# A two-layer expert kernel: side work placed by a count of two engines' time per chunk, and put off a chunk behind a step that feeds the other engine

## The chip, the core and the metric

The kernel runs on one core of a Trainium2 chip. The metric is the device time of one execution in microseconds, from a median of three runs. The engines' names are those of the profile: PE (matmul; PEld is its weight load), DVE (VectorE), ACT (ScalarE), POOL (GpSimd), SP (SyncE, which issues the loads and stores here).

## What is computed

A causal convolution with 7 taps per head (softmaxed), and then two expert layers one after the other, on 8192 tokens of width 192 with a hidden width of 2048, all in float32:

```python
x = _attn_ref(x, weight)             # out[t] = sum_k softmax(weight)[head, k] * x[t - 6 + k]
h = x @ w_in1                        # layer 1
g = h * np.clip(h + 3.0, 0.0, 6.0) / 6.0
x = g @ w_out1
h = x @ w_in2                        # layer 2
g = np.where(h > 0.0, h, np.exp(np.minimum(h, 0.0)) - 1.0)
out = g @ w_out2
```

## The kernel before

**Blocks, layers and chunks.** The tokens are cut into 16 blocks of 512, the hidden width into 16 pieces of 128. A chunk is one piece of one block in one layer, so there are 2 x 16 x 16 = 512 chunks; the code calls them slots (line 578 on) and counts them from 0, and so does this text. The first 32 chunks are layer 1 of blocks 0 and 1, then come blocks 2 to 6 of layer 1 up to chunk 111, and from 112 on a block of layer 2 and a block of layer 1 take turns; from chunk 416 on (blocks 10 to 15) only layer 2 is left. In the code `l` is 0 for layer 1 and 1 for layer 2. Chunk 32 is `BOTH`.

**A chunk's main work.** `mm1` (line 511) makes h = x @ w_in in a PSUM bank; there are three such banks. Float32 values are split in a high and a low part, so x stands as the operands opA (high), opB (low) and opC and opD (the last 64 of the 192 rows, high and low). `gate` (line 535) makes u on ACT and g on DVE; in layer 2 ACT runs twice (u, then its exponential). `split_g` (line 550) makes gh on ACT and gl on DVE, the two parts of g. `mm2` (line 559) adds g @ w_out to accumulators, five chunks later. On ACT and DVE a chunk begins with its u or g, and then holds gh or gl of the chunk before.

**Two streams.** Up to chunk 35 each matmul uses all 128 rows. From chunk 36 (`BOTH + LAG`) on the lower 64 rows and the upper 64 rows of the matmul engine are fed separately, by two generators whose matmuls are emitted alternately (lines 876 to 911); the lower half begins h, the upper half ends it 8 matmuls later. A half takes 10 matmuls for an even chunk and 9 for an odd one, and the other way for the other half. The lower half of chunk s + 3 writes the bank of chunk s, and so waits until g of chunk s has read it. From chunk 36 on the engines execute in the order in which the code emits, within each engine (`tc.manual_schedule`).

**Side work.** All else that ACT and DVE do is split into jobs: decoding and splitting the weights of both layers (`prepare`), the convolution of the later blocks with its taps and the making of opA to opD (`conv`), the split of layer 2's operand (`split_y`), and the sums and stores of results (`second_sum`, `store`). Each is a generator that yields after a step. `run_jobs(s)`, called once a chunk behind gl, first takes every step of a job that is at its last chunk, and then lets each job gain a rate (work left by chunks left) and takes steps while the sum of the gains is over `STEP` (300 units). A unit is about a nanosecond; the class `Meter` counts them for each engine. A step that yields `LATER` is one whose result the other engine needs: from chunk 128 on (`at[0, RA, 0]`) its job takes no further step in that chunk, unless it is at its last chunk.

In `conv_r` (line 339) the steps are: two casts on ACT, two casts on ACT, two subtractions on DVE (opC and opD), `LATER`, and two copies on ACT that read what DVE made. In `split_y` (line 490) they are: the cast of opA on ACT; the cast of the last rows' high part on ACT and opB on DVE; a copy of that high part on ACT and the last rows' subtraction (yr) on DVE; and a copy on ACT that reads what DVE subtracted. `LATER` stands behind each of the first three.

Of the kernel before, what the change touches and what calls it, by code (L numbers as in the profile page):

```python
# [18 lines left out]
LAG = 4  # L19
LAG2 = LAG + 1  # L20
HEAD = 8
RA = 7
# [5 lines left out]
ACT_LOW = range(5, 9)  # L28
R_CUTS = ((4, 4, 8), (8,))
STEP = 300  # L30
NB = 512
HB = NB // 2
SQ = 32
# [23 lines left out]
def conv_moe_moe2(ctx: ExitStack, tc: tile.TileContext, x, weight, w_in1, w_out1, w_in2, w_out2, out):  # L57
# [28 lines left out]
    LO, UP, ALL = slice(0, R), slice(R, P), slice(0, P)  # L86
    NBLK = NT // NB

    vec, act = Meter(nc.vector, 80), Meter(nc.scalar, 90)
# [71 lines left out]
    def split_w(item, f):  # L161

        kind, l, a, e = item
        if kind == "out":
            v = f[:, :(e - a) * D].rearrange("p (f e) -> p f e", f=e - a)
            w = wo[l][:, a:e]
            act.copy(w[:, :, 0:D], v)
            yield  # L170
            for c0, c1, to in ((0, P, 2 * P), (P, D, D)):
                vec.tensor_tensor(out=w[:, :, to:to + c1 - c0], in0=v[:, :, c0:c1],
                                  in1=w[:, :, c0:c1].bitcast(F32), op=ALU.subtract)
            yield
            return
        w = {k: v[:, a * P:e * P] for k, v in wi[l].items()}
        if kind == "in":
            f = f[:, :(e - a) * P]
            act.copy(w["h"], f)
            yield  # L180
            vec.tensor_tensor(out=w["l"], in0=f, in1=w["h"].bitcast(F32), op=ALU.subtract)
        else:
            f = f[:, :(e - a) // 2 * P].rearrange("p (f c) -> p f c", c=P)
            r = w["r"].rearrange("p (f two c) -> p two f c", two=2, c=P)
            for k, h in enumerate((LO, UP)):
                act.copy(r[h, k], f[h])
            yield
            for k, h, o in ((0, LO, UP), (1, UP, LO)):
                vec.tensor_tensor(out=r[o, k], in0=f[h], in1=r[h, k].bitcast(F32), op=ALU.subtract)
        yield  # L190


# [168 lines left out]
    LATER = object()  # L361
# [225 lines left out]
    at = {sl: i for i, sl in enumerate(slots)}  # L587
# [17 lines left out]
    def step(jb, s):  # L605
        w = vec.work, act.work
        said = next(jb[2], jobs)
        done = said is jobs
        if said is LATER and s >= at[0, RA, 0]:
            jb[8] = s  # L610
        cost = vec.work - w[0] + (act.work - w[1]) // 5
        jb[4] += 1
        jb[6] += cost
        jb[7] -= cost
        if done:
            jobs.remove(jb)

    def load(item):
# [3 lines left out]
        lo = {"out": n + 160, "in": n + 80, "r": 2 * n + 160}[kind]  # L622
        return n // 2 + 80 + n + 80 + lo + (2 * n + 180) // 5

    def run_jobs(s):

        def last(jb):
            return jb[0]() - (1 if jb[0]() <= BOTH else 2)

        def rate(jb):  # L630
            if jb[3]:
                return max(jb[5] - jb[6], 0) / max(last(jb) - s, 1)
            need, most = 0, 0
            for k in range(ready[0], len(items)):
                need += load(items[k]) * (1 - min(steps[0], 3) / 4 if k == ready[0] else 1)
                most = max(most, need / max(due(items[k]) - LEAD - 1 - s, 1))
            return most

        for jb in sorted(jobs, key=lambda j: j[0]()):
            while jb in jobs and (s >= last(jb) or not jb[5] and jb[3] and s >= jb[1]):  # L640
                step(jb, s)
        for jb in jobs:
            if s >= jb[1]:
                jb[7] += rate(jb)
        while True:
            going = [j for j in jobs if s >= j[1] and s > j[8]]
            if sum(j[7] for j in going) <= STEP:
                break
            step(max(going, key=lambda j: j[7]), s)

    def whole(*gens):
        for g in gens:
# [5 lines left out]

    def due(item):
        kind, l, a, e = item  # L660
        return at[l, 0, a] + ((LAG, LAG2 - 2)[l] if kind == "out" else 0)

    def when(i):

# [102 lines left out]
    for b in range(2, NBLK):  # L767
        e = at[0, b, 0] - 2
        if b <= RA:
            t = at[0, b - 1, 0]  # L770
            if b > 2:
                t, e = t - 2, e + (b < RA)
            else:
                t += NF // 2
        else:
            t = at[0, b - 1, 0] - 8
            e = at[0, b - 1, NF - 1]
        job(feed(b), 1, t - 8, t - 7)
        job(whole(squares(b), conv(b)), 2 + CONV, t, e, WORK["conv"])
    for b in range(NBLK):  # L780
        e = at[1, b, 0]
# [57 lines left out]
    BOTH = at[0, 2, 0]  # L839
# [55 lines left out]

    drain(whole_rows())
    with tc.manual_schedule():
        ends = {}
        n = {LO: 0, UP: HEAD}
        for half in (LO, UP):  # L900
            for s in range(BOTH + LAG, NS):
                assert half is LO or n[half] > ends[s]
                n[half] += 5 if (half is LO) == (slots[s][2] % 2 == 0) else 4
                if half is LO:
                    ends[s] = n[half]
                n[half] += 5 * (s >= BOTH + LAG2)
        going = [lower_rows(), upper_rows()]
        while going:
            for g in list(going):
                if next(g, jobs) is jobs:  # L910
                    going.remove(g)
        for k in range(B):
            drain(mm2(NS - 1, ALL, (0, 1, 3), slice(k * HB, (k + 1) * HB)))
        last_store(NBLK - 1, *(acc.pop((1, NBLK - 1, up)) for up in (False, True)))
        run_jobs(NS + 9)
# [30 lines left out]
```

## Time and profile before

| what | value |
|---|---|
| time, median of 3 runs (1141.54 to 1142.05) | 1141.55 us |
| the profiled execution, its own time | 1141.55 us |
| its span, first to last instruction | 1139.7 us |
| granted clock of PE, mean | 0.999 |
| PE busy | 1127.6 us (99%) |
| DVE busy | 918.5 us (81%) |
| ACT busy | 935.1 us (82%) |

Busy time of PE is modelled, since matmuls overlap. The list of waits says for each engine whom it waited for, and the timeline gives single instructions in order of time, with the idle time ahead of one in brackets and who ended it. The second number of a row of the timeline is the instruction's own duration; on DVE and ACT the next one can start before its end.

### The profile page before, as it was taken

How to read it: one execution, taken by the hardware profiler on the slowest of the kernel's cores; microseconds unless marked ns; L12 is line 12 of the kernel's file. 1: busy time of each engine (PE TensorE's matmuls, PEld its weight loads, DVE VectorE, ACT ScalarE, POOL GpSimd, SP SyncE). 2: the span in 40 equal slices, each digit the busy share in tenths (PEclk: the TensorE clock that was granted, in tenths of full speed). 3: DMA queues.
4: the chain of work that ended last, by engine and by line, in shares of the span. 5: the costliest groups of instructions: out<-in, count | busy, mean ns of one | idle time of the engine just before them, and what ended most of it. 6: DMA issues, size and time to landing. Idle time of an engine off the chain costs nothing.

```text
span 1139.7 us, 25118 instructions
## 1 busy us (share of the span) xinstructions
PE 1127.6 (99%) x9490; PEld 1065.4 (93%) x9490; DVE 918.5 (81%) x1558; ACT 935.1 (82%) x1699; POOL 44.5 (4%) x491
## 2 busy tenths in 40 slices
PE   8999999999999999999999999999999999999998
PEld 6787989888899999999999999999999999999997
DVE  7998999998887868779687887878867677777675
ACT  8877877778878787887878878787886899899886
POOL 0000000000000000000000000000000000000000
PEclk9999999999999999999999999999999999999999
DMA  6411121010010100101001010000000000000001
GB/s 188 108 53 42 36 49 44 29 29 1 2 29 1 21 10 2 29 1 29 2 7 23 1 29 1 16 15 1 16 1 15 2 1 16 15 15 15 9 7 28
DMA packets 105369, 26.79 MB, mean 24 GB/s; under 512 B 96416, under 2 KB 104096, under 8 KB 105248
## 3 DMA queue, kind: packets, MB, share of 16 engines
q1 hardware_dynamic: 104960, 24.99, 10.3%
q8 instruction: 74, 1.21, 0.4%
q14 instruction: 47, 0.39, 0.1%
q10 hardware_dynamic: 288, 0.20, 0.1%
HBM read 18.87 MB, written 6.29 MB: 22 GB/s over the span
## 4 chain that ended last, share of the span: by engine, by line
PE 92%; ACT 4%; DVE 3%; issue 1%; DMA 0%; ACTq 0%; SPq 0%; DVEq 0%
PE p L573 48%; PE h L527 44%; ACT u L51 1%; DVE g L51 1%; DVE gl L51 1%; DVE acc L51 0%; ACT gh L51 0%; ACT opC L51 0%; ACT xw L51 0%; ACT opD L51 0%; ACT diagl L51 0%; ACT xT L51 0%; DMA x_sq<-in_x_dram 0%; ACT acc L51 0%; DVE s L51 0%
## 5 line engine op out<-in xcount | busy, mean ns | idle before, releaser
L573 PE MATMUL p<-gh,wo 64*128 64x512 f32 (+1 forms) x2976 | 717.2, 386 | 0.0
L573 PE MATMUL p<-gl,wo 64*128 64x512 f32 (+2 forms) x1984 | 601.5, 386 | 0.0
L51 DVE SCALAR_TENSOR_TENSOR g<-u,h 128x512 f32<-128x512 f32 x512 | 350.4, 685 | 184.6 <-ACT u L51 178.2
L573 PEld LDWEIGHTS p<-gh,wo 64*128 64x128 f32 (+1 forms) x2976 | 412.9, 184 | 27.9 <-ACT gh L51 1.1
L51 DVE TENSOR_TENSOR gl<-g,gh 128x512 fp32r<-128x512 f32 x512 | 350.5, 685 | 1.9 <-ACT gh L51 1.6
L51 ACT CAST gh<-g 128x512 fp32r<-128x512 f32 x512 | 311.9, 609 | 9.6 <-DVE g L51 9.2
L51 ACT ACTIVATE u<-h,three 128x512 f32<-128x512 f32 x256 | 176.1, 688 | 107.7 <-PE h L527 105.3
L573 PEld LDWEIGHTS p<-gl,wo 64*128 64x128 f32 (+2 forms) x1984 | 252.6, 160 | 6.7 <-DVE gl L51 0.2
L51 ACT ACTIVATE u<-h 128x512 f32<-128x512 f32 x256 | 152.7, 597 | 57.5 <-PE h L527 56.2
L527 PE MATMUL h<-opA,wi1l 64*128 64x512 f32 x512 | 198.0, 387 | 0.0
L527 PE MATMUL h<-opA,wi1h 64*128 64x512 f32 x512 | 197.9, 386 | 0.0
L527 PE MATMUL h<-opB,wi1h 64*128 64x512 f32 x512 | 197.6, 386 | 0.0
L527 PE MATMUL h<-opA,wi0h 64*128 64x512 f32 (+1 forms) x476 | 183.9, 390 | 2.4 <-DVE g L51 2.1
L527 PE MATMUL h<-opA,wi0l 64*128 64x512 f32 (+1 forms) x476 | 183.3, 388 | 0.0
L527 PE MATMUL h<-opB,wi0h 64*128 64x512 f32 (+1 forms) x476 | 182.7, 387 | 0.0
L51 ACT ACTIVATE u<-u 128x512 f32<-128x512 f32 x256 | 161.9, 633 | 7.6
L527 PE MATMUL h<-opC,wi1r 64*128 64x512 f32 x384 | 148.2, 386 | 0.0
L527 PE MATMUL h<-opD,wi1r 64*128 64x512 f32 x384 | 148.2, 386 | 0.0
L527 PE MATMUL h<-opC,wi0r 64*128 64x512 f32 (+1 forms) x366 | 141.0, 387 | 0.7 <-ACT opC L51 0.6
L527 PE MATMUL h<-opD,wi0r 64*128 64x512 f32 (+1 forms) x366 | 140.8, 387 | 0.0
L51 DVE SCALAR_TENSOR_TENSOR acc<-xT,taps,acc 128x256 f32<-128x256 f32 (+1 forms) x180 | 106.8, 603 | 0.1
L527 PEld LDWEIGHTS h<-opA,wi0h 64*128 64x128 f32 (+1 forms) x476 | 87.6, 184 | 11.3 <-DVE g L51 6.5
(108 smaller groups left out, 1220.5 us busy)
## 6 DMA issues: line engine op xcount, KB each, us to landing
raw<-in_moe_w_out_dram SPq DMA_DIRECT2D x16, 384.0 KB, 3.2
out_dram<-z SPq DMA_DIRECT2D x180, 32.0 KB, 1.7
x_sq<-in_x_dram SPq DMA_DIRECT2D x112, 32.0 KB, 2.1
raw<-in_moe_w_in_dram SPq DMA_DIRECT2D x7, 512.0 KB, 3.9
raw<-in_moe_w_in_dram SPq DMA_DIRECT2D x8, 256.0 KB, 4.0
xr_sq<-in_x_dram SPq DMA_DIRECT2D x56, 32.0 KB, 2.1
x_sb<-in_x_dram SPq DMA_DIRECT2D x4, 128.0 KB, 2.9
raw<-in_moe_w_in_dram SPq DMA_DIRECT2D x4, 128.0 KB, 3.2
```

The costliest lines, as they stand in the source:

```text
L51: return fn(*args, **kw)
L527: mm = nc.tensor.matmul(h, k, m[half], start=low and i == 0, stop=high and i == len(todo) - 1)
L573: nc.tensor.matmul(p[:n, cols], k[:, :n], m[half, cols], start=first and not end and k is not w0l, stop=end == 1 and (last and cols.stop = ...
```

## The change

Five things are changed. `booked` counts for DVE and for ACT the units of a chunk, with what is over a chunk's 2153 (`SLOT`) carried on, and `full` stops the second loop of `run_jobs` once either has that much; the first loop, for jobs at their last chunk, does not ask it. `LATER` counts from chunk 36 on and not from 128. The weights of layer 2 are due 12 chunks earlier (`SOON`). The two subtractions of a wi1r item become two steps. And `run_jobs` runs once more, for chunk 35, at the head of the two streams.

```diff
--- before.py
+++ after.py
@@ -28,6 +28,8 @@
 ACT_LOW = range(5, 9)
 R_CUTS = ((4, 4, 8), (8,))
 STEP = 300
+SLOT = 2153
+SOON = 12
 NB = 512
 HB = NB // 2
 SQ = 32
@@ -187,6 +189,8 @@
             yield
             for k, h, o in ((0, LO, UP), (1, UP, LO)):
                 vec.tensor_tensor(out=r[o, k], in0=f[h], in1=r[h, k].bitcast(F32), op=ALU.subtract)
+                if l == 1 and k == 0:
+                    yield
         yield
 
 
@@ -606,7 +610,7 @@
         w = vec.work, act.work
         said = next(jb[2], jobs)
         done = said is jobs
-        if said is LATER and s >= at[0, RA, 0]:
+        if said is LATER and s >= BOTH + LAG:
             jb[8] = s
         cost = vec.work - w[0] + (act.work - w[1]) // 5
         jb[4] += 1
@@ -621,6 +625,11 @@
         n = (e - a) * {"out": D, "in": P, "r": R}[kind]
         lo = {"out": n + 160, "in": n + 80, "r": 2 * n + 160}[kind]
         return n // 2 + 80 + n + 80 + lo + (2 * n + 180) // 5
+
+    booked = [(e, [0, 0]) for e in (vec, act)]
+
+    def full(s):
+        return s >= BOTH + LAG and any(b[0] + e.work - b[1] >= SLOT for e, b in booked)
 
     def run_jobs(s):
 
@@ -636,6 +645,8 @@
                 most = max(most, need / max(due(items[k]) - LEAD - 1 - s, 1))
             return most
 
+        for e, b in booked:
+            b[:] = max(b[0] - SLOT, 0) + e.work - b[1] if s >= BOTH + LAG else 0, e.work
         for jb in sorted(jobs, key=lambda j: j[0]()):
             while jb in jobs and (s >= last(jb) or not jb[5] and jb[3] and s >= jb[1]):
                 step(jb, s)
@@ -644,9 +655,11 @@
                 jb[7] += rate(jb)
         while True:
             going = [j for j in jobs if s >= j[1] and s > j[8]]
-            if sum(j[7] for j in going) <= STEP:
+            if sum(j[7] for j in going) <= STEP or full(s):
                 break
             step(max(going, key=lambda j: j[7]), s)
+        for e, b in booked:
+            b[:] = b[0] + e.work - b[1], e.work
 
     def whole(*gens):
         for g in gens:
@@ -658,7 +671,7 @@
 
     def due(item):
         kind, l, a, e = item
-        return at[l, 0, a] + ((LAG, LAG2 - 2)[l] if kind == "out" else 0)
+        return at[l, 0, a] + ((LAG, LAG2 - 2)[l] if kind == "out" else 0) - l * SOON
 
     def when(i):
 
@@ -895,6 +908,7 @@
 
     drain(whole_rows())
     with tc.manual_schedule():
+        run_jobs(BOTH + LAG - 1)
         ends = {}
         n = {LO: 0, UP: HEAD}
         for half in (LO, UP):
```

The matmuls stand in the same order. What moves on ACT and DVE, first at chunk 442 to 445. ACT before, from u of chunk 442 (u twice, gh, then opC copied from opD) to u of chunk 445:

```order
L51 ACTIVATE u<-h 128x512
L51 ACTIVATE u<-u 128x512
L51 CAST gh<-g 128x512
L51 CAST opC<-opD 64x512
L51 ACTIVATE u<-h 128x512
L51 ACTIVATE u<-u 128x512
L51 CAST gh<-g 128x512
L51 ACTIVATE u<-h 128x512
L51 ACTIVATE u<-u 128x512
L51 CAST gh<-g 128x512
L51 CAST opD<-opC 64x512
L51 ACTIVATE u<-h 128x512
```

ACT now, from u of chunk 443:

```order
L53 ACTIVATE u<-h 128x512
L53 ACTIVATE u<-u 128x512
L53 CAST gh<-g 128x512
L53 CAST opD<-yr 64x512
L53 ACTIVATE u<-h 128x512
L53 ACTIVATE u<-u 128x512
L53 CAST gh<-g 128x512
L53 CAST opC<-opD 64x512
L53 CAST opD<-opC 64x512
L53 ACTIVATE u<-h 128x512
```

The copy of opD from opC has moved next to the copy of opC from opD, into chunk 444. DVE there, before, chunks 442 to 444:

```order
L51 SCALAR_TENSOR_TENSOR g<-u,h 128x512
L51 TENSOR_TENSOR gl<-g,gh 128x512
L51 TENSOR_TENSOR opC<-yr,opD 64x512
L51 SCALAR_TENSOR_TENSOR g<-u,h 128x512
L51 TENSOR_TENSOR gl<-g,gh 128x512
L51 SCALAR_TENSOR_TENSOR g<-u,h 128x512
```

Now, from g of chunk 443 to g of chunk 445:

```order
L53 SCALAR_TENSOR_TENSOR g<-u,h 128x512
L53 TENSOR_TENSOR gl<-g,gh 128x512
L53 TENSOR_TENSOR opB<-y_10208,opA 128x512
L53 SCALAR_TENSOR_TENSOR g<-u,h 128x512
L53 TENSOR_TENSOR gl<-g,gh 128x512
L53 TENSOR_TENSOR opC<-yr,opD 64x512
L53 SCALAR_TENSOR_TENSOR g<-u,h 128x512
```

The subtraction opC, which lies between the two copies of ACT, has moved from chunk 442 to chunk 444. The same holds 16 and 32 chunks earlier and 16, 32 and 48 later, with opC and opD exchanged at every second one; at 412 the first cast of the high part stands in chunk 410.

The second place is chunks 139 to 141, where the convolution of block 8 (64x256, acc) and the split of layer 2's block 1 (64x512, yr) end. ACT before, from u of chunk 139:

```order
L51 ACTIVATE u<-h,three 128x512
L51 CAST gh<-g 128x512
L51 ACTIVATE u<-h,three 128x512
L51 CAST gh<-g 128x512
L51 CAST opC<-opD 64x512
L51 ACTIVATE u<-h,three 128x512
L51 CAST gh<-g 128x512
L51 CAST opD<-opC 64x256
L51 CAST opC<-opD 64x256
L51 ACTIVATE u<-h,three 128x512
```

Now, from the casts behind u and gh of chunk 139:

```order
L53 CAST opD<-acc_4439 64x256
L53 CAST opC<-acc_4439 64x256 x2
L53 CAST opD<-acc_4439 64x256
L53 ACTIVATE u<-h,three 128x512
L53 CAST gh<-g 128x512
L53 CAST opC<-yr 64x512
L53 CAST opD<-opC 64x512
L53 CAST opC<-opD 64x512
L53 ACTIVATE u<-h,three 128x512
L53 CAST gh<-g 128x512
L53 CAST opD<-opC 64x256
L53 CAST opC<-opD 64x256
```

The four casts of the convolution have come into chunk 139, and the last copies of both splits now follow what they read from at once.

DVE there, before, from opB of chunk 138 to g of chunk 140:

```order
L51 TENSOR_TENSOR opB<-acc_4229,opA 128x512
L51 TENSOR_TENSOR opD<-yr,opC 64x512
L51 SCALAR_TENSOR_TENSOR g<-u,h 128x512
L51 TENSOR_TENSOR gl<-g,gh 128x512
L51 TENSOR_TENSOR opC<-acc_4231,opD 64x256
L51 TENSOR_TENSOR opD<-acc_4231,opC 64x256
L51 SCALAR_TENSOR_TENSOR g<-u,h 128x512
```

Now, from g of chunk 140 to g of chunk 142:

```order
L53 SCALAR_TENSOR_TENSOR g<-u,h 128x512
L53 TENSOR_TENSOR gl<-g,gh 128x512
L53 TENSOR_TENSOR opB<-y_1230,opA 128x512
L53 TENSOR_TENSOR opD<-yr,opC 64x512
L53 SCALAR_TENSOR_TENSOR g<-u,h 128x512
L53 TENSOR_TENSOR gl<-g,gh 128x512
L53 TENSOR_TENSOR opC<-acc_4439,opD 64x256
L53 TENSOR_TENSOR opD<-acc_4439,opC 64x256
L53 SCALAR_TENSOR_TENSOR g<-u,h 128x512
```

The subtraction opD on yr and the copy from it were two chunks apart and are in chunk 140; opC and opD on acc and the copies from them were two chunks apart and are in chunk 141.

The third place is the first chunks of the two streams. DVE before, chunks 37 and 38:

```order
L51 SCALAR_TENSOR_TENSOR g<-u,h 128x512
L51 TENSOR_TENSOR gl<-g,gh 128x512
L51 SCALAR_TENSOR_TENSOR acc_1149<-xT_1096,taps,acc_1149 128x512
L51 TENSOR_TENSOR yr<-s_1223,yr 64x512
L51 SCALAR_TENSOR_TENSOR g<-u,h 128x512
L51 TENSOR_TENSOR gl<-g,gh 128x512
L51 SCALAR_TENSOR_TENSOR acc_1151<-xT_1118,taps,acc_1151 128x256
L51 TENSOR_TENSOR wi1r<-xw,wi1r 64x4x128 x2
L51 SCALAR_TENSOR_TENSOR g<-u,h 128x512
```

Now, from gl in chunk 36 to g of chunk 39:

```order
L53 TENSOR_TENSOR gl<-g,gh 128x512
L53 SCALAR_TENSOR_TENSOR acc_1149<-xT_1096,taps,acc_1149 128x512
L53 TENSOR_TENSOR wi1r<-xw,wi1r 64x4x128
L53 SCALAR_TENSOR_TENSOR g<-u,h 128x512
L53 TENSOR_TENSOR gl<-g,gh 128x512
L53 TENSOR_TENSOR yr<-s_1231,yr 64x512
L53 SCALAR_TENSOR_TENSOR acc_1151<-xT_1119,taps,acc_1151 128x256
L53 SCALAR_TENSOR_TENSOR g<-u,h 128x512
L53 TENSOR_TENSOR gl<-g,gh 128x512
L53 SCALAR_TENSOR_TENSOR acc_1149<-xT_1096,taps,acc_1149 128x512
L53 TENSOR_TENSOR wi1r<-xw,wi1r 64x4x128
L53 SCALAR_TENSOR_TENSOR g<-u,h 128x512
```

One wi1r subtraction has moved from chunk 38 to chunk 36, and yr and the taps have changed places.

At chunks 60, 76, 92 and 121 opC and opD on acc stood on DVE before, with the copies from them on ACT in the same chunk at the first three; they stand at 61, 77, 93 and 124 now, with the copies in the same chunk at all four. At 77 and 124 opB stands right ahead of them. The same pairs stood two or three chunks apart at 171, 203 and so on up to 363 and 365, and are in one chunk now (173, 205, 237, 269, 301, 333 and 365).

## Rows read from the trace of the kernel before

**Rows 1.** Busy time by stretch, core 0: us, PE, PEld, DVE, ACT, POOL, PEclk, DMA, GB/s

```profile
99.00:309.00 210.00, 208.12 (x1811) 183.39 (x1812) 191.42 (x342) 167.38 (x311) 8.79 (x96) 1.00 0.12 28
309.00:1128.00 819.00, 819.00 (x7230) 803.81 (x7228) 631.79 (x1021) 681.92 (x1216) 33.45 (x380) 1.00 0.07 12
```

**Rows 2.** Waits, 99 to 309 us: engine, line, waited for, total us, times, longest

```profile
PEld h L527 <- DVE g L51: 5.5, 10, 1.2
...
ACT opD L51 <- DVE opC L51: 3.5, 3, 1.2
```

**Rows 3.** Timeline of PE: start us, us, engine, line, op, tiles; eight first matmuls

```profile
106.69 0.39 PE L527 MATMUL h<-opA,wi0h 64*128 64x512 f32 x1
...
116.73 0.39 PE L527 MATMUL h<-opA,wi0h 64*128 64x512 f32 x1
...
155.49 0.39 PE L527 MATMUL h<-opA,wi0h 64*128 64x512 f32 x1
...
165.30 0.39 PE L527 MATMUL h<-opA,wi0h 64*128 64x512 f32 x1
...
395.62 0.39 PE L527 MATMUL h<-opA,wi0h 64*128 64x512 f32 x1
...
981.33 0.39 PE L527 MATMUL h<-opA,wi1h 64*128 64x512 f32 x1
...
983.60 0.39 PE L527 MATMUL h<-opA,wi1h 64*128 64x512 f32 x1
...
989.94 0.39 PE L527 MATMUL h<-opA,wi1h 64*128 64x512 f32 x1
```

**Rows 4.** Timeline of PE at chunk 64 (in brackets: idle before, by whom ended)

```profile
160.82 0.50 PE L527 MATMUL h<-opA,wi0h 64*128 64x512 f32 x1 [0.80 <-DVE g L51]
...
161.16 0.40 PE L527 MATMUL h<-opB,wi0h 64*128 64x512 f32 x1
```

**Rows 5.** Timeline of DVE, chunks 60 and 61

```profile
156.82 0.69 DVE L51 SCALAR_TENSOR_TENSOR g<-u,h 128x512 f32<-128x512 f32 x1 [1.26 <-ACT u L51]
...
158.03 0.41 DVE L51 TENSOR_TENSOR opC<-acc,opD 64x256 fp32r<-64x256 f32 x1
...
160.08 0.69 DVE L51 SCALAR_TENSOR_TENSOR g<-u,h 128x512 f32<-128x512 f32 x1 [0.53 <-ACT u L51]
```

**Rows 6.** Timeline of ACT, chunks 60 to 62

```profile
158.47 0.41 ACT L51 CAST opD<-opC 64x256 fp32r<-64x256 f32 x1 [1.18 <-DVE opC L51]
...
159.35 0.69 ACT L51 ACTIVATE u<-h,three 128x512 f32<-128x512 f32 x1
...
160.45 0.69 ACT L51 ACTIVATE u<-h,three 128x512 f32<-128x512 f32 x1
```

**Rows 7.** Timeline of ACT, chunks 441, 442, 444 and 445

```profile
977.95 0.60 ACT L51 ACTIVATE u<-h 128x512 f32<-128x512 f32 x1
...
980.15 0.59 ACT L51 ACTIVATE u<-h 128x512 f32<-128x512 f32 x1
...
984.30 0.60 ACT L51 ACTIVATE u<-h 128x512 f32<-128x512 f32 x1
...
986.10 0.62 ACT L51 CAST opD<-opC 64x512 fp32r<-64x512 f32 x1
986.74 0.60 ACT L51 ACTIVATE u<-h 128x512 f32<-128x512 f32 x1
```

**Rows 8.** Timeline of DVE, chunks 442 and 445

```profile
981.43 0.69 DVE L51 SCALAR_TENSOR_TENSOR g<-u,h 128x512 f32<-128x512 f32 x1
...
982.64 0.68 DVE L51 TENSOR_TENSOR opC<-yr,opD 64x512 fp32r<-64x512 f32 x1
...
988.04 0.69 DVE L51 SCALAR_TENSOR_TENSOR g<-u,h 128x512 f32<-128x512 f32 x1 [1.16 <-ACT u L51]
```

**Rows 9.** Timeline of DVE, chunks 37 and 38

```profile
105.73 0.69 DVE L51 SCALAR_TENSOR_TENSOR g<-u,h 128x512 f32<-128x512 f32 x1 [0.86 <-ACT u L51]
...
110.14 1.39 DVE L51 TENSOR_TENSOR wi1r<-xw,wi1r 64x512 fp32r<-64x512 f32 x2
```

## Prediction

> **What bounds the kernel now.** I read the busy time by stretch first, then the waits of the matmul engine, then its cadence, then the order in time around one wait. From 309 us to 1128 us PE is busy in all of 819.00 us, and from 99 us to 309 us it has 1.88 us idle, with DVE at 191 of 210 us [rows 1]. So the end is set by PE's count of matmuls, which the change leaves as it is, and by the moments at which PE waits. [rows 2] says who makes it wait in the two streams: g on DVE (5.5 us of weight-load waits), and ACT in turn stands 3.5 us in three waits for a DVE result, opC.
>
> The cadence gives what is lost. The first matmul of chunk 172's lower half starts at 395.62, that of chunk 444 at 981.33: 272 chunks in 585.71 us, 2.1533 us each [rows 3]. At the same rate the 404 chunks from chunk 40 (106.69) would take 869.95 us; they took 874.64. So **4.69 us are lost in the two streams**, all of it before chunk 172: 1.43 from chunk 40 to 44 (10.04 us for 4 chunks), 1.20 from chunk 62 to 66 (9.81), the other 2.06 in the rest. That is the most that better placed side work can give: 0.41%.
>
> How one loss comes about stands in [rows 4 to 6], chunk 60. ACT has u and gh done, then wants to copy opD from opC. DVE makes opC only after g and gl: g at 156.82, opC at 158.03 for 0.41 us. ACT stands 1.18 us, starts the copy at 158.47 (0.03 us after opC's end), and the next u follows at 159.35: **2.53 us after g**. That delays g of chunk 61 to 160.08, its end to 160.77, and the lower half of chunk 64, which needs the same bank of the three, starts at 160.82, 0.05 us later. After it the next matmul comes 0.34 us on where the cadence is 0.23 (2.1533 over 9.5 matmuls): a restart of some 0.12 us with every stall.
>
> How much lateness PE bears: g of chunk 445 starts at 988.04 for 0.69 us, and the bank is wanted by chunk 448 at 989.94 [rows 3, 8]: 1.21 us. That u was itself 0.17 us late (2.44 us after the one before, where an even chunk takes 981.33 to 983.60, 2.27 us [rows 3, 7]). So an odd chunk of layer 2 has 1.21 + 0.17 - 0.05 = **1.33 us to spare**. In layer 1 g comes 0.73 us after u (159.35 to 160.08) and not 1.30 (986.74 to 988.04): 1.33 + 0.56 = 1.89 for odd chunks, and 0.23 more, 2.12, for even ones, since an odd chunk takes 2.04 (two take 4.31).
>
> **The change part by part.** It issues the same instructions: the matmuls stand in the same order, and one pair of the wi1r subtractions is parted. What moves is side work on DVE and ACT, and some loads on SP's queue; the list of which [rows 2] are two lines names no DMA in that stretch: nothing for these.
>
> *Chunks 36 to 43.* Before, DVE waits 0.86 us for u of chunk 37, since ACT has two wi1r casts and another in chunk 36, and then two wi1r subtractions (1.39 us) stand together in chunk 38 [rows 9]. Now ACT has nothing but u and gh in chunk 36. DVE's chunks 36 to 38 hold other steps of the same size: one wi1r each in 36 and 38, a wide tap where a narrow one and a decode stood. So g of chunk 39 comes the 0.86 us earlier, and of the 1.43 us some 0.5 stay; 0.1 to 0.6 is open, and I take **0.4**.
>
> *The couplings of blocks 3 to 6.* The step that feeds ACT is put off a chunk, but a step at its last chunk is taken whatever was said, and so only the one of chunk 43 becomes free. Those of chunks 60, 76 and 92 come back at 61, 77 and 93. At 61 and 93 u is 2.53 us after g where it would be 2.04 - 0.73 = 1.31: 1.22 us late, with 0.1 to 0.5 brought along, under 2.12: nothing, so that the 1.20 us behind chunk 60 goes. At 77 opB stands ahead of opC (0.60 more): 3.13 - 1.31 = 1.82 late, with 0 to 0.6 of DVE's own; then chunk 78 holds g, gl, wi1r and a transpose (3 x 0.60 + 0.70 = 2.5 us against 2.27): 2.1 to 2.7 late against 1.89. I take the middle, 0.5, and a restart: **0.6 us**.
>
> *The booked count.* It stops side work at 2153 units a chunk, but what is due is put in all the same, so DVE's sum over chunks 62 to 71 stays 0.1 to 0.2 us a chunk over the slot. From the 1.3 us of chunk 62 it may reach the 1.89 at chunk 67: 0 to 0.6, taken as **0.3**.
>
> *Chunk 124 (layer 2).* Block 7's opB, opC, opD and both copies from them now stand in one chunk: u is 3.13 us after g, where it would be 2.27 - 1.30 = 0.97. 2.16 - 1.33 = 0.83, and a restart: **0.9 us**.
>
> *Chunks 140 and 141.* Before, no ACT copy there waits for its own chunk's DVE step. Now chunk 139 has four half-width copies on ACT, 1.10 (159.35 to 160.45, u and gh) + 4 x 0.44 (158.47 to 159.35 has two) = 2.86 us against 2.04: 0.82 late. Chunk 140 has opB, a full-width opD on DVE and the copy from it: 0.60 + (1.21 + 0.68 + 0.03 + 0.64) = 3.16 us from g to u [rows 7, 8], where 2.27 - 0.73 = 1.54 is normal: 2.44 late against 1.89. Chunk 141 adds 2.53 - 1.31: 3.66 late against 2.12. PE loses 1.54 us and two restarts: **1.8 us**.
>
> *The last six blocks.* For blocks 10 to 15 the split of layer 2's operand stood in chunks 441, 442 and 444 (and 16 further on or back): DVE's opC at 982.64, ACT's copy from it at 986.10, two chunks later, and nobody waits. Now DVE's subtraction, the copy that it needs next to it and the copy from its result are all in chunk 444; their sizes stand in [rows 7, 8]. u of chunk 445 comes 1.21 + 0.68 + 0.03 + 0.64 = 2.56 us after g, where 0.97 is normal: 1.59 late. The high part's copy in chunk 443 adds 0.16 (2.20, as from 977.95 to 980.15, against 2.04) in chunks 444 and 476; in 428, 460 and 492 it is of the 0.64 us kind (986.10 to 986.74) and not of the 0.52 us one, 0.28; in 412 none. Less 1.33 that is 0.42 twice, 0.54 three times and 0.26: 2.7 us, and six restarts, 0.7: **3.4 us in a stretch that loses nothing now**.
>
> *Seven more* (173, 205, ... 365) put opC, opD and their copies in one chunk: 1.22 + 0.3 late against 2.12, nothing.
>
> **The sum.** 0.4 + 0.6 + 0.3 + 0.9 + 1.8 + 3.4 = 7.4 us lost after, 4.69 before: +2.7 us. The profiled execution took 1141.55 us, 1.85 more than its span of 1139.7, and that is the median of the three runs too. 1141.55 + 2.7 = **1144.3 us**, slower by 0.24%. The ends: each of the ten new or kept stalls 0.15 us kinder, and the three open terms at their lower ends, make 5.0 lost and 1141.9; each 0.2 us longer, and the open terms at their upper ends, make 10.2 and 1147.0.
>
> **Rivals.** *The late six fit.* Their lateness, 1.59 to 1.87, is over the spare 1.33 by only 0.26 to 0.54. If DVE and ACT are some 0.3 us quicker there (gl does not wait for gh, the copy's start overlaps), most of these stalls go with their restarts: 3.4 falls to 0.5, 4.5 lost in all, 1141.55 - 0.2 = 1141.4: not slower. It decides from some 0.25 us a chunk on. Against it: the 2.53 us chain shows no such overlap. *The wait for a result goes away.* If a put-off step bought its chunk everywhere, as the change says, all but some 1 us of the 4.7 goes: 1141.55 - 3.7 = 1137.9, faster. Against it: the built order has opC and its copy in one chunk at 61, 77, 93, 124 and 141. *DVE's steps do not overlap.* If a step behind a wait on another engine starts only at the end of the one ahead, 0.69 apart and not 0.60, each chain is 0.17 to 0.26 longer; over the ten stalls that is 2 us more: 1146.3. Against it: from g at 981.43 to opC at 982.64, with gl between, are two steps of 0.60 us, though the instructions take 0.69 [rows 8].
>
> [...]
>
> **How the numbers follow.** A measurement of this kernel tells about 0.2%, 2.3 us, from no change. The forecast's case (the late six stall as worked out) has 0.66, the six that fit 0.22, the gain 0.05, the longer chains 0.07. The forecast's own range is 1142.4 to 1146.2 and lies on both sides of the bound at 1143.8; I give 0.45 of its 0.66 to slower. With the longer chains slower has 0.52, faster 0.04, the rest 0.44. The range takes in half of the six that fit and the longer chains' lower part: 1141.3 to 1146.2.
>
> **What would show it.** In the changed kernel's trace: waits of ACT for DVE's opC or opD, some nineteen of 0.7 to 2 us and not three; PE waits for g at about 921, 955, 990, 1025, 1060 and 1095 us, each some 0.4 us, where PE has none now; two close together at about 336 us, 0.5 and 1 us; the wait for u of chunk 37 gone; PE's wait for g of chunk 61, 0.80 us at 160.82, gone [rows 4]. The forecast is wrong if PE is busy without a gap from 400 us on, or if the lateness at 139 to 141 is taken up by DVE having begun opC earlier than its place in the order says. If the late six show and the total is still level, the early part has gained more than I allow.

## The result: 0.62% slower, and the profile after

The changed kernel takes **1148.88 us** (median of 6 runs, 1148.45 to 1149.78) and the kernel before 1141.85 (6 runs, 1141.54 to 1142.84): a ratio of 1.0062, interval 1.0049 to 1.0075. The prediction had the side right and the size not: 1144.3, with 1146.2 as its upper end. The profiled execution took 1148.89 us, its span is 1147.2.

PE's busy time and the busy time by stretch (the columns of [rows 1]) are these; the first line is of the page, the other two of the view by stretch:

```profile
PE 1132.0 (99%) x9490; PEld 985.3 (86%) x9490; DVE 916.8 (80%) x1558; ACT 933.5 (81%) x1699; POOL 44.4 (4%) x491
```

```profile
99.00:309.00 210.00, 207.70 (x1797) 190.71 (x1797) 187.01 (x332) 164.02 (x304) 8.60 (x95) 1.00 0.11 26
309.00:1128.00 819.00, 816.15 (x7180) 708.50 (x7178) 629.67 (x1023) 676.47 (x1210) 33.25 (x377) 1.00 0.07 12
```

Before, PE had no idle time in the second stretch [rows 1]; now it has 2.85 us. DVE and ACT do the same work. The waits changed as a list shows, first of 99 to 317 us, then of 317 to 1136 (engine, line, waited for, total us, times, longest):

```profile
PEld h L531 <- DVE g L53: 5.1, 10, 1.4
ACT opD L53 <- DVE opC L53: 4.7, 4, 1.4
ACT wo L53 <- DVE xw L53: 2.9, 2, 2.5
PE h L531 <- DVE g L53: 1.6, 3, 0.9
PEld h L531 <- ACT opC L53: 1.1, 2, 0.9
...
ACT opD L53 <- DVE opC L53: 12.5, 15, 1.2
PEld h L531 <- DVE g L53: 6.3, 8, 1.1
ACT opC L53 <- DVE opD L53: 4.5, 7, 0.9
```

Where [rows 2] had three waits of ACT for opC there are 26 now for opC or opD, 22 of them after 317 us; 19 take 0.79 to 1.43 us, which are the prediction's "some nineteen", and the rest under 0.3. Two kinds the prediction did not have: ACT for the decoded weight xw, and PE for the operand opC itself.

**Where the time went.** PE's timeline gives the first matmul of the lower half at chunks 40, 44, 72, 84, 96, 104, 130, 148, 412 and 498, which answers to [rows 3]:

```profile
107.10 0.39 PE L531 MATMUL h<-opA,wi0h 64*128 64x512 f32 x1
...
116.23 0.39 PE L531 MATMUL h<-opA,wi0h 64*128 64x512 f32 x1
...
177.00 0.39 PE L531 MATMUL h<-opA,wi0h 64*128 64x512 f32 x1
...
204.69 0.39 PE L531 MATMUL h<-opA,wi0h 64*128 64x512 f32 x1
...
231.19 0.39 PE L531 MATMUL h<-opA,wi0h 64*128 64x512 f32 x1
...
250.17 0.39 PE L531 MATMUL h<-opA,wi0h 64*128 64x512 f32 x1
...
307.00 0.39 PE L531 MATMUL h<-opA,wi0h 64*128 64x512 f32 x1
...
347.53 0.39 PE L531 MATMUL h<-opA,wi1h 64*128 64x512 f32 x1
...
916.15 0.39 PE L531 MATMUL h<-opA,wi1h 64*128 64x512 f32 x1
...
1105.07 0.39 PE L531 MATMUL h<-opA,wi1h 64*128 64x512 f32 x1
```

Each difference less 2.15335 us a chunk (585.71 / 272, the prediction's rate) is what that stretch lost: 231.19 to 250.17, say, are 18.98 us for 8 chunks that need 17.23, so 1.75. The table has the same for before and for the profiled execution of each experiment; the last column is the median of the timed runs. The loss is more than PE's idle time in the views, which counts from the modelled end of the matmul before and leaves out the slow restart: at chunk 448, shown below, it is 0.19 us where the loss is 0.53, and the matmul from opB behind it comes 0.34 us on (995.21 to 995.55), where in the pair before the stall it came 0.22 on (994.38 to 994.60). The spans of the two profiles differ by 7.5 us: 7.05 are this loss, and 0.4 lie before chunk 0, where the programs are the same. In all 14 profiles chunk 0 begins between 13.55 and 14.66 us; from there to chunk 40 all 14 take 93.08 to 93.18 us, so that spread is no work of the change, and the lost time is compared first and the medians second.

| us lost in chunks | 40-44 | 44-72 | 72-84 | 84-96 | 96-104 | 104-130 | 130-148 | 148-412 | 412-498 | sum | median |
|---|---|---|---|---|---|---|---|---|---|---|---|
| before | 1.42 | 1.21 | 0.64 | 0.51 | 0.13 | 0.78 | 0 | 0 | 0 | 4.68 | 1141.85 |
| predicted | 0.4 | 0.3 | 0.6 | 0 | 0 | 0.9 | 1.8 | 0 | 3.4 | 7.4 | 1144.3 |
| after | 0.52 | 0.47 | 1.85 | 0.66 | 1.75 | 0.85 | 1.77 | 0.13 | 3.72 | 11.73 | 1148.88 |
| e1 late steps put off early, alone | 1.43 | 0.63 | 0.07 | 0.52 | 0 | 0.81 | 0 | 0 | 0 | 3.44 | 1140.58 |
| e2 no count | 0.52 | 0 | 0.73 | 0 | 0.40 | 0.91 | 0 | 0 | 0 | 2.55 | 1140.19 |
| e3 bound 2500 | 0.57 | 0.02 | 0.85 | 0.07 | 0 | 1.07 | 0.04 | 0 | 0 | 2.62 | 1139.50 |
| e4 layer 2's split early | 0.57 | 0.51 | 1.88 | 1.72 | 0.11 | 0.79 | 1.40 | 0 | 0 | 6.98 | 1144.18 |
| e5 six coupled in before | 1.42 | 1.18 | 0.63 | 0.52 | 0.17 | 0.79 | 0 | 0 | 4.37 | 9.08 | 1146.68 |
| e6 conv parted | 0.53 | 0.64 | 0.70 | 0.22 | 0 | 0 | 0.75 | 0 | 3.74 | 6.57 | 1144.00 |
| e7 weights parted | 0.03 | 0.43 | 1.81 | 0.31 | 0.03 | 0.78 | 1.73 | 0.05 | 3.80 | 8.96 | 1145.96 |
| e8 bound 2350 | 0.57 | 0.61 | 0.59 | 0.07 | 0.07 | 0.10 | 0.35 | 0 | 0 | 2.36 | 1140.14 |
| e9 count alone | 0 | 1.29 | 1.27 | 1.23 | 2.09 | 7.44 | 7.72 | 0.13 | 3.78 | 24.95 | 1160.31 |
| e10 weights not early | 0.03 | 0.66 | 0.94 | 0.27 | 0 | 2.70 | 6.56 | 0.12 | 3.78 | 15.06 | 1154.27 |
| e11 wi1r parted, alone | 0.77 | 1.79 | 0.63 | 1.84 | 0.13 | 0.79 | 0 | 0 | 0 | 5.93 | 1143.32 |
| e12 all three mended | 0 | 0 | 0.27 | 0.91 | 0 | 0.29 | 0.28 | 0 | 0 | 1.74 | 1138.73 |

**One of the six late stalls**, chunks 444 to 448 of the timelines of ACT, DVE and PE:

```profile
991.11 0.62 ACT L53 CAST opC<-opD 64x512 fp32r<-64x512 f32 x1
992.53 0.62 ACT L53 CAST opD<-opC 64x512 fp32r<-64x512 f32 x1 [0.80 <-DVE opC L53]
993.17 0.60 ACT L53 ACTIVATE u<-h 128x512 f32<-128x512 f32 x1
```

```profile
990.62 0.69 DVE L53 SCALAR_TENSOR_TENSOR g<-u,h 128x512 f32<-128x512 f32 x1
...
991.82 0.68 DVE L53 TENSOR_TENSOR opC<-yr,opD 64x512 fp32r<-64x512 f32 x1
994.47 0.69 DVE L53 SCALAR_TENSOR_TENSOR g<-u,h 128x512 f32<-128x512 f32 x1 [1.97 <-ACT u L53]
```

```profile
995.21 0.50 PE L531 MATMUL h<-opA,wi1h 64*128 64x512 f32 x1 [0.19 <-DVE g L53]
...
995.55 0.40 PE L531 MATMUL h<-opB,wi1h 64*128 64x512 f32 x1
```

u of chunk 445 comes 2.55 us after g of 444 (the prediction said 2.56), g follows 1.30 later and ends at 995.16, and PE starts 0.05 after it. In [rows 7, 8] the copy from opC stood two chunks after it, and PE ran through.

**Two stalls that were not forecast as they came.** Chunk 96 on ACT and DVE, and PE at chunk 100:

```profile
238.73 0.51 ACT L53 CAST wo<-xw 128x384 fp32r<-128x384 f32 x1 [2.52 <-DVE xw L53]
...
239.59 0.67 ACT L53 ACTIVATE u<-h,three 128x512 f32<-128x512 f32 x1
```

```profile
236.98 0.65 DVE L53 SCALAR_TENSOR_TENSOR g<-u,h 128x512 f32<-128x512 f32 x1
237.55 0.68 DVE L53 TENSOR_TENSOR gl<-g,gh 128x512 fp32r<-128x512 f32 x1
238.15 0.55 DVE L53 SCALAR_TENSOR_TENSOR xw<-xw,cw 128x384 int32<-128x384 int32 x1
...
240.30 0.69 DVE L53 SCALAR_TENSOR_TENSOR g<-u,h 128x512 f32<-128x512 f32 x1 [1.33 <-ACT u L53]
```

```profile
241.04 0.49 PE L531 MATMUL h<-opA,wi0h 64*128 64x512 f32 x1 [0.93 <-DVE g L53]
```

It is the same coupling in another job: DVE's decoding step and the ACT copy from it stand in one chunk, and u behind the copy comes 2.61 us after g, 1.30 later than the prediction's normal 1.31. That alone would fit in its 2.12 us to spare. But g of chunk 96 was late already: it ended at 237.63, and PE took that bank for chunk 99 at 237.88, so only 0.20 us of the 2.12 were left (0.25 less the hand-over of 0.05). And chunk 80, the first of block 5, on ACT and on PE:

```profile
195.26 0.41 ACT L53 CAST opD<-opC 64x256 fp32r<-64x256 f32 x1 [1.43 <-DVE opC L53]
195.72 0.40 ACT L53 CAST opC<-opD 64x256 fp32r<-64x256 f32 x1
```

```profile
196.17 0.50 PE L531 MATMUL h<-opC,wi0r 64*128 64x512 f32 x1 [0.48 <-ACT opC L53]
...
197.90 0.39 PE L531 MATMUL h<-opA,wi0h 64*128 64x512 f32 x1
```

PE waits here for the copies of chunk 77 themselves: chunk 80 multiplies by opC, which is ready at 196.12. Chunk 81 begins at 197.90, 1.07 us late.

### The profile page after: what moved, and what is told of

Same layout as the page of the kernel before. It is cut to its first block, busy times and chain, and to the rows that moved or that the text cites. A ratio compares the mean times of both kernels' runs of the same rounds, so it can differ in the third digit from the quotient of the medians.

```text
span 1147.2 us, 25110 instructions
## 1 busy us (share of the span) xinstructions
PE 1132.0 (99%) x9490; PEld 985.3 (86%) x9490; DVE 916.8 (80%) x1558; ACT 933.5 (81%) x1699; POOL 44.4 (4%) x491
## 3 DMA queue, kind: packets, MB, share of 16 engines
q8 instruction: 74, 1.21, 0.4%
## 4 chain that ended last, share of the span: by engine, by line
PE 92%; ACT 4%; DVE 3%; issue 1%; ACTq 0%; DVEq 0%
PE p L577 47%; PE h L531 44%; ACT u L53 2%; DVE g L53 1%; DVE gl L53 1%; PE psc L330 1%; ACT opC L53 0%; DVE opD L53 0%; ACT opD L53 0%; ACT gh L53 0%; DVE opC L53 0%; DVE acc L53 0%; ACT xw L53 0%; ACT xT L53 0%; DVE wi1r L53 0%
## 5 line engine op out<-in xcount | busy, mean ns | idle before, releaser
L577 PE MATMUL p<-gh,wo 64*128 64x512 f32 (+1 forms) x2976 | 708.2, 387 | 0.1
L577 PE MATMUL p<-gl,wo 64*128 64x512 f32 (+2 forms) x1984 | 591.1, 386 | 0.0
L577 PEld LDWEIGHTS p<-gh,wo 64*128 64x128 f32 (+1 forms) x2976 | 391.9, 184 | 45.5 <-ACT gh L53 1.1
L577 PEld LDWEIGHTS p<-gl,wo 64*128 64x128 f32 (+2 forms) x1984 | 241.2, 160 | 25.4 <-DVE gl L53 0.2
L531 PEld LDWEIGHTS h<-opA,wi1h 64*128 64x128 f32 x512 | 94.2, 184 | 12.7 <-DVE g L53 6.3
L53 DVE SCALAR_TENSOR_TENSOR acc<-xT,taps,acc 128x256 f32<-128x256 f32 (+1 forms) x180 | 104.2, 601 | 0.1
```

Of the source, the lines that this page charges most:

```text
L53: return fn(*args, **kw)
L531: mm = nc.tensor.matmul(h, k, m[half], start=low and i == 0, stop=high and i == len(todo) - 1)
L577: nc.tensor.matmul(p[:n, cols], k[:, :n], m[half, cols], start=first and not end and k is not w0l, stop=end == 1 and (last and cols.stop = ...
```

## The experiments

**Is it the count, or the early put-off?** The theory: the bound holds steps back till the last chunk of their job, where they are taken together. e1 is the kernel before with one line changed; e2 is the changed kernel in which the bound is never reached; e3 has `SLOT = 2500`.

```diff
-        if said is LATER and s >= at[0, RA, 0]:
+        if said is LATER and s >= BOTH + LAG:
```

> The kernel before with one part of the change: a step that says 'a chunk later' is put off from the start of the two streams on (chunk 36) and not from chunk 128 on; no booked count, no parting of the wi1r pair, no earlier weights. Theory (the count is at fault): without the count a step is taken when its rate asks for it, well ahead of its last chunk, so the put-off gets its chunk everywhere: no ACT copy waits for opC of its own chunk at 60, 76, 92, PE's 1.2 us behind chunk 60 go, the 1.4 us of chunks 36 to 43 stay: 1139.0 to 1140.6 us, faster than before. Rival (the early put-off itself is what costs): waits of ACT for opC at 61, 77 and 93 as in the changed kernel and losses at 80 to 83 and 97 to 102: 1143 to 1146 us.

```diff
-        return s >= BOTH + LAG and any(b[0] + e.work - b[1] >= SLOT for e, b in booked)
+        return False and any(b[0] + e.work - b[1] >= SLOT for e, b in booked)
```

> The changed kernel without its booked count (the bound is never reached; the put-off from chunk 36, the parted wi1r pair and the earlier weights stay). Theory (the count holds rated steps back to their last chunk, where the DVE step and the copy from it are taken together): all the couplings go, and with them the losses at 416 to 496 (3.7 us), 144 to 146 (1.8), 128/129 (0.8), 97 to 102 (1.7) and most of 80 to 83 (1.7); what is left is 1 to 2.5 us: 1138.5 to 1140.5 us, faster than before. Rival (put-off early): the losses before chunk 128 stay, about 5 us: 1143.5. Rival (bunched work: wherever the steps go, a chunk of DVE or ACT overflows): new stalls of the same sum, 1146 to 1149.

> The changed kernel with one number changed: the bound of the booked count is 2500 a chunk and not 2153, which is its length at the pace of the matmuls. Theory (the bound as such makes the couplings, since layer 1's conv and sums fill it): with 16% more room no copy stands in one chunk with the DVE step before it, and the time is that of the kernel without the count, 1138.5 to 1140.5 us. Rival (it is not the bound, but that steps are counted and taken in another order): 1147 to 1149 us.

All three are faster than before: 1140.58 (ratio 0.9989, 0.9980 to 0.9998), 1140.19 (0.9985, 0.9976 to 0.9994) and 1139.50 us (0.9979, 0.9970 to 0.9988). What e2's trace leaves of the list of waits from 99 to 309 us, as far as PE waits for DVE's g, and of the stretch behind it:

```profile
PEld h L531 <- DVE g L53: 2.7, 5, 0.8
PE h L531 <- DVE g L53: 0.6, 2, 0.4
```

```profile
309.00:1128.00 819.00, 819.00 (x7230) 803.82 (x7228) 631.79 (x1021) 681.78 (x1217) 33.45 (x380) 1.00 0.07 12
```

No wait of ACT for opC or opD of the same chunk is left in either stretch, and PE is busy in all of the second. So the count makes the couplings, and costs 11.73 - 2.55 = 9.2 us; the early put-off alone gains 1.24. e3 says that it is the bound's size. How 2153 is filled can be counted from `Meter` (512 units and 90 for a full-width step of ACT, 80 for one of DVE): a chunk of layer 2 has three such steps on ACT, 1806 units, and one copy more makes 2408; in layer 1 conv and sums fill DVE or ACT. The rated steps then wait, and the loop for last chunks takes them without asking.

**Is a copy behind its own chunk's DVE step the whole price?** e4 lets the split of layer 2's operand begin two chunks ahead of its last one, a step a chunk (`jb[3]` is a job's number of steps; layer 1's sums have 4 too, so its line frees them as well, and the last six blocks have none of these); e5 has no count, and makes only the six late couplings in the kernel before.

```diff
             while jb in jobs and (s >= last(jb) or not jb[5] and jb[3] and s >= jb[1]
+                                  or jb[3] == 4 and s > jb[8] and s >= last(jb) - 2):
```

> The changed kernel, count and all; only the split of layer 2's operand is taken from two chunks ahead of its last chunk on, a step a chunk where it says 'later', and no more all at once in the last chunk. Theory (each late stall is a DVE step and the ACT copy from it in one chunk): the six stalls at 416 to 496 go, 3.7 us, and at 144 the part that chunk 140 adds, 0.5 to 1.0 us; the conv's couplings at 77, 124 and 141 stay with their losses: 1144.0 to 1145.0 us. Rival (PE waits there since ACT or DVE have too much in the chunk, wherever the steps stand): the six stalls move to the chunks beside and stay: 1148 to 1149 us.

```diff
         vec.tensor_tensor(out=lo[h], in0=yr[h], in1=hi[h].bitcast(F32), op=ALU.subtract)
-        yield LATER
+        if b < 10:
+            yield LATER
```

> The kernel before, with no count and nothing else of the change; only for blocks 10 to 15 the split of layer 2's operand has its last put-off taken out, so that DVE's subtraction and the ACT copy from it stand in one chunk (410, 426, ... 490) and not in two. Theory (a copy behind its own chunk's DVE step is the whole price): six stalls of PE at chunks 414, 430, ... 494, 0.4 to 0.8 us each with the restart, 3.4 to 4.5 us in all: 1145.3 to 1146.3 us, and the couplings of 60, 76, 92 as before. Rival (the late steps of the changed kernel cost since the DVE step, the copy before it and the forced chunk come on top of each other, and a lone coupling fits in the slack of 1.33 us): 1141.9 to 1142.9 us.

In e4 the six stalls are gone (3.72 to 0). The sum fits the expectation, but not term by term: 144 to 146 gave back only 0.37 of the 0.5 to 1.0, and the weight's coupling of chunk 96 moved to 80 in the built order, which saves 1.64 at 96 to 104 and costs 1.06 at 84 to 96. The early sums of layer 1 moved it: with the line narrowed to the split, the code emits that step at 96 as before. In e5 six stalls appear out of nothing: 4.37 us, at the upper end of the expectation (its median is 0.4 above it). One of them, on ACT and PE:

```profile
985.48 0.62 ACT L51 CAST opD<-opC 64x512 fp32r<-64x512 f32 x1 [0.80 <-DVE opC L51]
986.13 0.60 ACT L51 ACTIVATE u<-h 128x512 f32<-128x512 f32 x1
```

```profile
988.16 0.50 PE L528 MATMUL h<-opA,wi1h 64*128 64x512 f32 x1 [0.19 <-DVE g L51]
```

The rows repeat those of chunk 444 above: the same 0.80 us on ACT, the same 0.19 on PE. A coupling in an even chunk of layer 2 is enough by itself. In an odd chunk of layer 1 it is not: ACT waits 1.18 us in each of the seven pairs from 173 on, and chunks 148 to 412 lose 0.13 us in all.

**What are the losses before chunk 148?** e6 parts the conv's steps (the line of e4 with `jb[3] > 8` and `last(jb) - 1`); e7 parts the weights' (with `not jb[3]`, `last(jb) - 1`, and the second `yield` of `decode` saying `LATER`). That `LATER` does nothing, in e7 or in e12: `decode` runs inside `counted`, which yields nothing on, so `run_jobs` never sees it. What e7 really does is to take the weights' last steps one chunk earlier; in its trace no copy of a weight stands in one chunk with its xw any more.

> The changed kernel, count and all; only the conv's job may be taken from one chunk ahead of its last chunk on, up to its 'later', so that opC and opD on DVE and the ACT copies from them stand in two chunks in every block. The split of layer 2's operand stays as it is. Theory: ACT no longer waits for opC at 61, 77, 93, 124, 141, and the losses at 80 to 83 (1.7 us, of which 1.07 are PE waiting for the operand itself), at 128/129 (0.8) and most of 144 to 146 (1.8) go, and with the other order of the weights those of 97 to 102 (1.7); the six late stalls (3.7 us) stay: 6.0 us lost, 1143.2 us, 1142.5 to 1144.2. Rival (the early losses come from DVE's side work being too much for chunks 62 to 102, whatever the coupling): 4 us of them stay, 1146 to 1147 us.

> The changed kernel, count and all; only the weights' job says 'later' after DVE's second step of the decode (xw) and may be taken from one chunk ahead of its last chunk on, so that the ACT copy of the decoded weight stands a chunk behind xw. Theory (the 2.5 us wait of ACT for xw in chunk 96 is what costs 1.7 us at chunks 100 to 102): these go, the conv's and the split's couplings stay, those before chunk 96 within 0.5 us: 1146.7 to 1147.7 us. Rival (chunks 97 to 102 lose time by DVE's sum of weights, conv and sums): the loss stays within 0.5 us, 1148.4 to 1149.4 us.

e6: 72 to 84 falls from 1.85 to 0.70, the wait of PE for opC is gone, and 104 to 130 from 0.85 to 0. 130 to 148 falls from 1.77 to 0.75, the part of chunk 140, which is the split's. What stays at 72 to 84 is g of chunk 77, which ends at 194.94, late behind opB, opC and opD on DVE in chunk 76, while chunk 80 starts at 194.99. The weight's coupling moved here too, from 96 to 61 (ACT waits 1.09 us), and 96 to 104 lose nothing. e7: 96 to 104 falls from 1.75 to 0.03. It gained a further 1 us that was not expected: 0.5 at chunks 40 to 44, 0.35 at 84 to 96. The weights' steps move there too, and which of them made room was not tried singly. The conv's coupling of chunk 93 went as well, against the expectation. It is not what costs at 96 to 104: in e4 it stands at 93 with the same 1.18 us of ACT's wait, and that stretch loses 0.11.

**Can the bound be chosen?** e8 has `SLOT = 2350`.

> The changed kernel with the bound of the count at 2350 a chunk: by the order, no copy stands in one chunk with its DVE step, and DVE's sum in chunks 72 to 96 and 110 to 128 is kept flatter than with 2500. Theory (a bound a little over the pace parts the work and still flattens it): the losses at 75 to 77 (0.7 us) and 110 (0.2) that the bound of 2500 leaves go, 1.3 to 2.0 us lost in the two streams: 1138.6 to 1139.5 us. Rival (the count is of no use at any bound): as with 2500 or without it, 1139.5 to 1140.3 us.

It lost 2.36 us, as e2 and e3 did within 0.3, and not under 2.0: the crowded chunks moved from 110 and 129 in e3 to 60 and 133. The theory fell: between 2350 and no bound the time hardly depends on it. What is gained there is the couplings' absence and no flatter load.

**The other parts.** e9 is the kernel before with the count alone; e10 the changed kernel with `SOON = 0`; e11 the kernel before with the wi1r pair parted and nothing else.

> The kernel before with the booked count alone (bound 2153 from chunk 36 on); steps that say 'a chunk later' are put off from chunk 128 on only, the wi1r pair stands together and the weights have their old due times. Theory (the count is what costs, and the rest of the change makes it milder): the six late stalls and the one at 144 as in the changed kernel (4.5 to 5.5 us in all), and layer 2's weights, whose last steps now wait for their last chunk too, fall together with block 7's conv in chunks 124 and 141: from 124 to 146 some 8 to 11 us; 16 to 22 us lost in the two streams: 1153 to 1159 us. Rival (count and early put-off cost only together): 1142 to 1149 us.

> The changed kernel with the due times of layer 2's weights as before (not 12 chunks earlier); all else as changed. Theory (the earlier due times are a gain that the count hides): the weights' last step falls into chunks 124 to 141 on top of block 7's conv, 5 to 8 us more there, while chunk 96's wait of ACT for xw and the 1.7 us behind it go: 1151 to 1155 us. Rival (the earlier weights only crowd chunks 62 to 102): faster than the changed kernel, 1145 to 1147.5 us.

> The kernel before with nothing but the wi1r pair of subtractions parted into two steps. Theory (this part is worth what chunk 42 shows): 0.9 of the 1.43 us lost at 41 to 43 go; but one more step to be counted moves the next ones, so that copies stand behind their own chunk's DVE step at 44 and 90 besides 60, 76 and 92: 0 to 2 us more there: 1141.0 to 1143.0 us. Rival (a part without a price of its own): 1140.6 to 1141.2 us.

The count alone costs 20.3 us (24.95 - 4.68): so the other parts had hidden more than half of its price. The 12 chunks by which layer 2's weights are due earlier are the main cover: without them 104 to 148 loses 9.26 us and not 2.62, since the weights' last steps meet block 7's conv (1.8 of it by the clock, as the section on the hardware shows). e9 came out 3 us over the expected loss; the same section says why. e10's profiled execution took 1151.9 us and the three others 1154.3 to 1154.4. Their mean granted clock was 0.996 and not 0.998; as an estimate, 0.002 of 1152 us are 4.6 us more at a clock of 0.50, 2.3 us lost. Where they fell is not shown, since they have no trace. Parting the wi1r pair gave 0.65 at chunks 40 to 44 and cost 1.9 elsewhere, since one more step shifts the later ones: copies came to stand at 44 and 90 behind their chunk's DVE step, 0.3 us over the upper end of what was expected.

**A version that is faster than both.** e12 is the changed kernel with a bound that seldom binds (2700), `SOON = 8`, and the weights' last steps taken two chunks earlier.

```diff
-SLOT = 2153
-SOON = 12
+SLOT = 2700
+SOON = 8
...
-        yield
+        yield LATER
...
+                                  or not jb[3] and s > jb[8] and s >= last(jb) - 2):
```

> The changed kernel with a bound of 2700 and not 2153, layer 2's weights due 8 chunks earlier and not 12, and the weights' job parted behind xw and allowed from two chunks ahead of its last on. No copy stands in a chunk with its DVE step, chunks 36 to 42 have room as in the run with the weights parted (where nothing was lost at 42). Theory: 1.0 to 2.0 us lost in the two streams, 1138.3 to 1139.3 us, the fastest of all. Rival (moving the weights shifts the crowding to other chunks, as every other change did): 2.4 to 3.5 us lost, 1139.5 to 1140.8 us.

1138.73 us (0.9971, 0.9960 to 0.9983), 1.74 us lost: as expected. In its trace no copy of opC, of opD or of a weight stands in one chunk with its DVE step. What each of the three gives was not run singly. Its two stretches:

```profile
99.00:309.00 210.00, 209.82 (x1839) 183.51 (x1839) 193.15 (x345) 170.10 (x316) 8.86 (x97) 1.00 0.12 28
309.00:1128.00 819.00, 819.00 (x7228) 675.28 (x7226) 629.63 (x1021) 680.89 (x1215) 33.74 (x379) 1.00 0.07 12
```

## Why the prediction was right in direction and wrong in size

- **The bound, and the cadence.** Right: from chunk 148 to 412 the changed kernel lost 0.13 us in 568, and the losses elsewhere are PE's stalls.
- **Chunks 36 to 43** (0.4) lost 0.52, **the booked count at 62 to 71** (0.3) 0.47, **chunk 124** (0.9) 0.85, **140 and 141** (1.8) 1.77: within 0.2 each. Chunks 61 and 93 cost nothing, as said, and so do the seven pairs from 173 on.
- **The last six blocks** (3.4) lost 3.72, by the chain that the prediction worked out (2.55 us for its 2.56); e4 takes it away and e5 makes it from nothing.
- **Chunk 77** (0.6) lost 1.85, and here a step failed. The prediction priced a late copy by one reader only, the u behind it and the bank three chunks on. It has a second: the copies are the operand of chunk 80. PE waited for that first, 1.06 us of the 1.85, and this wait went in e6. The bank's share, forecast as the 0.6, was 0.44 at chunks 82 and 83: g of 79 ended at 200.20, and PE began chunk 82 at 200.25.
- **The missing term.** Chunks 96 to 104 lost 1.75 us of which the sum has nothing. The list of couplings was made from jobs that say `LATER`, conv and split. The weights' job never says it, but its decode (DVE) and its copy (ACT) are coupled the same way, and the built order had them side by side in chunk 96. e7 takes it away, and in e4 the loss moves with the coupling. The rule for the price failed here too: by it 1.30 us late of 2.12 is nothing. At 61 and 93 it allowed for 0.1 to 0.5 us brought along; here 1.92 was used up (2.12 less 0.20). The list of waits before, 99 to 309 us, had shown that this pair can wait, with its steps in chunks 70 and 71:

```profile
ACT wi1h L51 <- DVE xw L51: 0.9, 1, 0.9
```

- **Chunks 84 to 96** (nothing) lost 0.66, in two stalls at 86 and 94. The kernel before lost 0.51 there, part of the prediction's "other 2.06", and its sum for after has nothing in that place and gives no reason. In both stalls PE starts 0.05 to 0.06 us after a g that is late since DVE was busy without a gap: g of chunk 83 ends at 209.19 and chunk 86 begins at 209.25; g of chunk 91 ends at 226.69 and chunk 94 begins at 226.74. So here it is the sum of DVE's work and no copy. e6 and e7 each lower it to 0.2 or 0.3 without being made for it; which step made room there is not shown. Ahead of the first stall, chunk 82 holds three taps and a sum behind g and gl, and the g of 83 follows them:

```profile
207.91 0.69 DVE L53 SCALAR_TENSOR_TENSOR y<-p,y 128x512 f32<-128x512 f32 x1
208.51 0.68 DVE L53 SCALAR_TENSOR_TENSOR g<-u,h 128x512 f32<-128x512 f32 x1
```

- **The sum.** 7.4 was 11.73: 1.75 for the missing term, 1.25 for chunk 77, 0.66 for 84 to 96, and 0.65 over the others. The range failed with it, since its ends were the stalls on the list, each a little longer or shorter, with nothing for one that was not on it. The other 0.3 us of the miss lie in the base, 1141.55, where the median of before is 1141.85.
- **The rivals.** The late six did not fit. The wait did not go away, though e2 shows what the prediction's 1137.9 stood for: with the count out, couplings go and 2.1 us are gained. DVE's steps overlapped as before (990.62, then gl, then opC at 991.82: 0.60 a step), so the third rival's 1146.3, the nearest of the times, came from steps 0.69 apart, which this trace does not show.

## What to carry to other kernels

A limit on optional work does not lower the work: it moves it to the deadline, and if the deadline's loop ignores the spacing that the ordinary loop keeps, the limit undoes the spacing. When a built order is read for a producer and its consumer on two engines in one slot, go through every pair of tiles that crosses engines and not the jobs that the change names, and price each late result for all of its readers. A change of several parts is worth running one part at a time: here one part lost 9 to 20 us and one gained 1.2.

## What the hardware showed that was not expected

Three long stalls of PE cost more than their length. PE's timeline of e10 at chunks 128 and 145, and of e9 at the same two:

```profile
300.70 0.49 PE L531 MATMUL h<-opA,wi0h 64*128 64x512 f32 x1 [2.35 <-DVE g L53]
...
342.42 0.50 PE L531 MATMUL h<-opA,wi1h 64*128 64x512 f32 x1 [3.20 <-DVE g L53]
```

```profile
306.57 0.79 PE L528 MATMUL h<-opA,wi0h 64*128 64x512 f32 x1 [4.03 <-DVE g L52]
...
351.07 0.79 PE L528 MATMUL h<-opA,wi1h 64*128 64x512 f32 x1 [3.22 <-DVE g L52]
```

Busy time by stretch behind these (the number behind POOL's is the granted clock), first e10's, then e9's:

```profile
302.00:304.00 2.00, 2.00 (x20) 1.73 (x18) 1.62 (x4) 1.95 (x5) 0.09 (x1) 1.00 0.00 0
...
342.40:343.40 1.00, 0.98 (x8) 0.85 (x10) 0.89 (x2) 0.99 (x3) 0.00 (x0) 1.00 0.23 36
343.40:345.00 1.60, 1.60 (x10) 1.30 (x10) 1.42 (x3) 1.57 (x3) 0.09 (x1) 0.54 0.00 0
345.00:346.00 1.00, 1.00 (x8) 0.74 (x6) 0.83 (x2) 0.02 (x1) 0.00 (x0) 0.50 0.00 0
346.00:348.00 2.00, 2.00 (x16) 1.65 (x14) 0.00 (x0) 0.93 (x2) 0.09 (x1) 0.77 0.00 0
348.00:350.00 2.00, 2.00 (x20) 1.71 (x18) 1.29 (x2) 1.64 (x4) 0.09 (x1) 1.00 0.00 0
```

```profile
306.00:307.00 1.00, 0.43 (x2) 0.43 (x4) 1.00 (x2) 0.97 (x3) 0.00 (x0) 0.50 0.00 0
307.00:308.00 1.00, 1.00 (x6) 0.74 (x6) 0.62 (x2) 0.97 (x2) 0.00 (x0) 0.50 0.00 0
...
311.00:312.00 1.00, 1.00 (x8) 0.81 (x6) 0.00 (x0) 0.00 (x0) 0.00 (x0) 0.50 0.00 0
312.00:313.00 1.00, 1.00 (x10) 0.80 (x8) 0.18 (x1) 0.90 (x2) 0.04 (x1) 0.69 0.00 0
313.00:314.00 1.00, 1.00 (x12) 0.82 (x10) 1.00 (x2) 0.30 (x1) 0.05 (x1) 1.00 0.00 0
```

After 2.35 us idle the clock stayed at 1.00. After the 3.20 of e10 it was 0.54, 0.50 and 0.77 from 343.40 to 348 and then 1.00; after the 4.03 of e9 it stood at 0.50 from 306 to 312, was 0.69 up to 313 and then 1.00. A microsecond from 307 to 312 has 6 to 8 matmuls, that from 313 on has 12. Behind the 3.22 of e9 the first matmul takes 0.79 us, as behind the 4.03, where those of e10 take 0.49 and 0.50, and the mean clock from 340 to 360 us is 0.83. In e10 it fell only when PE had run again for a microsecond. Chunks 129 and 130 of e9 then lost 2.96 us with g ready 2.8 and 3.6 us ahead of its reader, and chunks 146 and 147 another 2.9 with g ready 2.6 and 3.9 us ahead: 5.9 of e9's 24.95 us, which is more than what it lost over its expectation. In e10 chunks 146 and 147 lost 1.76 us with g ready 1.75 and 3.25 us ahead.
